# A recurrent attention and FFN kernel: denominators by bank, a reordered first layer norm, one load for V, the last layer norm on another engine, other banks in the FFN

## The chip, the cores and the metric

The kernel runs on one core of one Trainium2 chip. The metric is the device time of one execution in microseconds (us); lower is better. The times quoted are medians of executions that the measurement calls fast. A ratio is the mean time of one kernel's fast runs over the mean time of the other's fast runs of the same rounds, so it is not quite the ratio of the medians that stand beside it. Traces are of single executions, and a number from a trace is a number of that execution.

## The reference, cut to what matters

One sequence of 2048 tokens, width 512. It is layer-normalised and cut into 64 segments of 32 tokens. Each segment attends, with 32 heads of 128, over itself and 8 memory rows, and the first 8 rows of its output are the memory of the next segment. So segments run strictly one after the other. A second layer norm and a gated FFN (512 to 1376 to 512, ReLU gate) follow.

```python
for s in range(n_seg):                                   # 64, serial
    h = jnp.concatenate([mem, xs], axis=1)               # 8 + 32 rows
    q = jnp.einsum('btd,dhe->bhte', h, Wq)               # k, v alike
    scores = jnp.einsum('bhqe,bhke->bhqk', q, k) * scale
    p = _softmax(jnp.where(mask, scores, -1e9))
    o = jnp.einsum('bhqk,bhke->bhqe', p, v)
    o = jnp.einsum('bhte,hed->btd', o, Wo)
    mem = o[:, :M, :].copy()
...
h = x + A(layernorm(x));  h2 = h + B(layernorm(h))       # B: (relu(gate) * up) @ W_down
```

## The kernel before

The program is written as one list of instructions for each engine, with waits on named events of other engines. An engine works through its own list in order, so the place of an instruction in its list matters as much as its waits. The five places below are those that the change touches (cuts are marked with `...`). `mm` is a TensorE matmul, `act` a ScalarE (ACT) instruction, `e_tt`/`e_stt`/`e_copy` are elementwise ones on VectorE (DVE) or GpSimd (POOL). A bank is one of the pieces of PSUM, the memory that matmuls write to; `psf(b, ...)` is bank b.

The start. Four chunks of 512 tokens are transposed, their sums and squares are formed on TensorE, and all chunks are normalised only after the last of them:

```python
for c in range(NCH):
    ...                                     # 16 transposes, copies to HT (ACT and DVE)
    e_tt("dve", SQ, src_all(c), src_all(c), ALU.mult, ...)
    ...                                     # 4 + 4 matmuls with ONES: sums, sums of squares
    act(A1, psf(bS1, 0, CH), ACT.Square, ..., scale=1.0 / D_MODEL)
    e_stt("dve", VV, psf(bS2, 0, CH), 1.0 / D_MODEL, A1, ALU.mult, ALU.subtract, ...)
    act(VV, VV, ACT.Ln, ...);  act(RB[c], VV, ACT.Exp, ..., scale=-0.5)
    e_stt("dve", MRB[c], psf(bS1, 0, CH), 1.0 / D_MODEL, RB[c], ALU.mult, ALU.mult, ...)
prev = [("dve", "1MR%d" % (NCH - 1))]
for c in range(NCH):
    for tau in range(4):                    # 2 x 4 x 4 = 32 DVE instructions
        e_tt("dve", TTb, src_tau(c, tau), RB[c], ALU.mult, ..., waits=prev)
        ...
```

The middle of a segment on TensorE. V is made in four chunks of 512 columns; its matmuls use half the array's columns each (`tile_position`), the others use the whole array:

```python
emit_v_chunk(0, ...);  emit_pairs(...)                   # V chunk 0, then the scores
emit_v_chunk(1, [("dve", "QE%db1" % s)])
for b in range(3):                                       # softmax denominators
    w = [("dve", "MK%db2" % s)] if b == 0 else []        # all behind the third mask
    mm(psf(b, 0, SCOLS[b]), ONES, EB[:, 480 * b:480 * b + SCOLS[b]], True, True,
       post=(("pe", "D%d" % s) if b == 2 else None), waits=w)
emit_v_chunk(2, [("dve", "QE%db2" % s)])
emit_v_chunk(3, [("dve", "VE%dc0" % s)])
...                                                      # O = P V (16), then Wo (128)
```

ACT makes the reciprocals as exp(-ln(x)), in two pieces (960 and 320 columns). DVE's list in a segment is: evict Q, evict V chunk 0, three masks, evict V chunks 1, 2 and 3, scale O by the reciprocals in three pieces, residual add. The FFN accumulates the first half of the down projection in banks 0 and 1 and then the second half in the same banks:

```python
for fc in range(NFC):
    for k, dc in enumerate((2, 3)):
        w = [("dve", "RA%d" % c)] if (fc == 0 and k == 0) else []   # banks 0, 1 must be read out
        mm(PSF[:, 512 * (dc - 2):512 * (dc - 2) + CH], WDv[...], HFFv[...], ...)
```

The second layer norm of each segment runs on GpSimd, one segment behind; that of the last segment has nothing to hide behind. The V weights are loaded in eight pieces that sort the heads into even and odd, in runs of 256 bytes.

The softmax here doesn't subtract the row's maximum and nothing guards it: scores larger than these inputs give would overflow.

Of the kernel before, what the change touches and what calls it, by code (L numbers as in the profile page):

```python
# [3 lines left out]
P = 128  # L4
# [9 lines left out]
SEGL = 32  # L14
# [60 lines left out]
def build_kernel(nc, A_x, A_mem0, A_Wq, A_Wk, A_Wv, A_Wo, A_seg_len, B_x, B_W_gate, B_W_up, B_W_down, out):  # L75
# [16 lines left out]
    with ExitStack() as es:  # L92
# [40 lines left out]
        WVv = WBUF[:, OFF_V:OFF_V + 16384].rearrange("p (t b q e) -> p t b q e", t=4, b=2, q=16)  # L133
# [82 lines left out]
        wv5 = A_Wv.rearrange("(t p) (q b) e -> t b p q e", p=P, b=2)  # L216
        for b in range(2):
            for tau in range(4):
                dma("sp", WVv[:, tau, b, :, :], wv5[tau, b], post=("d_wv", "w%d%d" % (b, tau)))
# [23 lines left out]
        for c in range(NCH):  # L243
            first = True
            for t_ in range(TPC):
                for tau in range(4):
                    w = []
                    if first:
                        w = [("d_x%d" % c, "x"), ("gp", "ID1")]
                        if c > 0:  # L250
                            w += [("act", "XTE%da" % (c - 1)), ("dve", "XTE%db" % (c - 1))]
                        first = False
                    tr(PSH[:, tau * 512 + t_ * 128:tau * 512 + t_ * 128 + 128],
                       xr_tiles(c)[:, t_, tau * 128:(tau + 1) * 128], ID[:, :],
                       post=(("pe", "XT%d" % c) if (t_ == TPC - 1 and tau == 3) else None), waits=w)
            act(HT[:, 0:2, c * CH:(c + 1) * CH],
                PSH[:, 0:1024].rearrange("p (t c) -> p t c", t=2)[:, :, 0:CH], ACT.Copy,
                post=("act", "XTE%da" % c), waits=[("pe", "XT%d" % c)])
            e_copy("dve", HT[:, 2:4, c * CH:(c + 1) * CH],
                   PSH[:, 1024:2048].rearrange("p (t c) -> p t c", t=2)[:, :, 0:CH],  # L260
                   post=("dve", "XTE%db" % c), waits=[("pe", "XT%d" % c)])
            par = c % 2
            bS1, bS2 = 2 * par, 2 * par + 1
            w = [("act", "XTE%da" % c), ("dve", "XTE%db" % c)]
            if c > 0:
                w.append(("pe", "1S2c%d" % (c - 1)))
            e_tt("dve", SQ[:, :, :], src_all(c), src_all(c), ALU.mult, post=("dve", "1SQ%d" % c), waits=w)
            for tau in range(4):
                w = []
                if tau == 0:  # L270
                    w = [("act", "XTE%da" % c), ("dve", "XTE%db" % c), ("gp", "ONE")]
                    if c >= 2:
                        w.append(("dve", "1MR%d" % (c - 2)))
                mm(psf(bS1, 0, CH), ONES[:, :], src_tau(c, tau), tau == 0, tau == 3,
                   post=(("pe", "1S1c%d" % c) if tau == 3 else None), waits=w)
            for tau in range(4):
                w = [("dve", "1SQ%d" % c)] if tau == 0 else []
                mm(psf(bS2, 0, CH), ONES[:, :], SQ[:, tau, :], tau == 0, tau == 3,
                   post=(("pe", "1S2c%d" % c) if tau == 3 else None), waits=w)
            w = [("pe", "1S1c%d" % c)]  # L280
            if c > 0:
                w.append(("dve", "1V%d" % (c - 1)))
            act(A1, psf(bS1, 0, CH), ACT.Square, post=("act", "1A1%d" % c), waits=w, scale=1.0 / D_MODEL)
            e_stt("dve", VV, psf(bS2, 0, CH), 1.0 / D_MODEL, A1, ALU.mult, ALU.subtract,
                  post=("dve", "1V%d" % c),
                  waits=[("pe", "1S2c%d" % c), ("act", "1A1%d" % c)])
            act(VV, VV, ACT.Ln, post=("act", "1L%d" % c), waits=[("dve", "1V%d" % c), ("gp", "EPS")],
                bias=EPSB[:, 0:1])
            act(RB[c], VV, ACT.Exp, post=("act", "1R%d" % c), waits=[("act", "1L%d" % c)], scale=-0.5)
            e_stt("dve", MRB[c], psf(bS1, 0, CH), 1.0 / D_MODEL, RB[c], ALU.mult, ALU.mult,  # L290
                  post=("dve", "1MR%d" % c), waits=[("act", "1R%d" % c)])
        prev = [("dve", "1MR%d" % (NCH - 1))]
        for c in range(NCH):
            for tau in range(4):
                e_tt("dve", TTb, src_tau(c, tau), RB[c], ALU.mult, post=("dve", "1T%dt%d" % (c, tau)),
                     waits=prev)
                o = XNT4[:, tau, c * SPC:(c + 1) * SPC, 0:32]
                e_tt("dve", o, TTb.rearrange("p (s c) -> p s c", c=32)[:, 0:SPC, :],
                     MRB[c].rearrange("p (s c) -> p s c", c=32)[:, 0:SPC, :], ALU.subtract,
                     post=("dve", "1N%dt%d" % (c, tau)), waits=[("dve", "1T%dt%d" % (c, tau))])  # L300
                prev = [("dve", "1N%dt%d" % (c, tau))]
        for tau in range(4):
# [36 lines left out]
        def emit_ln2_act_lr(q):  # L339
            i = q % 2  # L340
            w = [("gp", "V2%d" % q), ("gp", "EPS")]
# [6 lines left out]
        def emit_ln2_gp(q):  # L348
            i = q % 2
            e_tt("gp", M2SQ[i], MEAN2[i], MEAN2[i], ALU.mult, post=("gp", "V2a%d" % q),  # L350
                 waits=[("act", "CP2%d" % q)] + ([("gp", "N2%dt3" % (q - 1))] if q > 0 else []))
            e_tt("gp", VV2[i], EX2B[i], M2SQ[i], ALU.subtract, post=("gp", "V2%d" % q), waits=[("gp", "V2a%d" % q)])
            e_tt("gp", MR2b[i], MEAN2[i], R2b[i], ALU.mult, post=("gp", "MR2%d" % q),
                 waits=[("act", "R2%d" % q), ("gp", "V2%d" % q)])
            prev = [("gp", "MR2%d" % q)]
            for tau in range(4):
                e_tt("gp", TT2b[i], HT[:, tau, q * SEGL:(q + 1) * SEGL], R2b[i], ALU.mult,
                     post=("gp", "T2%dt%d" % (q, tau)), waits=prev)
                e_tt("gp", XNT4[:, tau, q, 0:32], TT2b[i], MR2b[i], ALU.subtract,
                     post=("gp", "N2%dt%d" % (q, tau)), waits=[("gp", "T2%dt%d" % (q, tau))])  # L360
                prev = [("gp", "N2%dt%d" % (q, tau))]

        for s in range(NSEG):
# [35 lines left out]
            def emit_v_chunk(cv, waits_first=()):  # L399
                vb = Vbank[cv]  # L400
                first = True
                for tau in range(4):
                    for b in range(2):
# [3 lines left out]
                           WVv[:, tau, b, 4 * cv:4 * cv + 4, :], tau == 0, tau == 3,  # L407
# [9 lines left out]
            emit_v_chunk(0, ([("d_wv", "w13")] if s == 0 else []) + [("dve", "QE%db0" % s)])  # L417
# [4 lines left out]
            for b in range(3):  # L422
                w = [("dve", "MK%db2" % s)] if b == 0 else []
                mm(psf(b, 0, SCOLS[b]), ONES[:, :], EB[:, 480 * b:480 * b + SCOLS[b]], True, True,
                   post=(("pe", "D%d" % s) if b == 2 else None), waits=w)
            emit_v_chunk(2, [("dve", "QE%db2" % s)])
            emit_v_chunk(3, [("dve", "VE%dc0" % s)])
# [29 lines left out]
            for b in range(3):  # L457
                act(EB[:, 480 * b:480 * b + SCOLS[b]], psf(b, 0, SCOLS[b]), ACT.Exp,
                    post=("act", "EX%db%d" % (s, b)), waits=[("pe", "S%db%d" % (s, b))], scale=SCALE)
            act(LR[:, 0:960].rearrange("p (b c) -> p b c", b=2), PSF3[:, 0:2, 0:480], ACT.Ln,  # L460
                post=("act", "LN%da" % s), waits=[("pe", "D%d" % s)])
            act(LR[:, 0:960], LR[:, 0:960], ACT.Exp, post=("act", "RC%da" % s), waits=[("act", "LN%da" % s)],
                scale=-1.0)
            act(LR[:, 960:1280], psf(2, 0, 320), ACT.Ln, post=("act", "LN%db" % s))
            act(LR[:, 960:1280], LR[:, 960:1280], ACT.Exp, post=("act", "RC%db" % s),
                waits=[("act", "LN%db" % s)], scale=-1.0)
# [5 lines left out]
            if last:  # L472
                emit_ln2_act(s)
                emit_ln2_act_lr(s)
# [26 lines left out]
            for b in range(3):  # L501
                w = [("pe", "O%db%d" % (s, b)), ("act", "RC%d%s" % (s, "a" if b <= 1 else "b"))]
# [12 lines left out]
            if last:  # L515
                emit_ln2_gp(s)
# [6 lines left out]
        def ffn_chunk(c):  # L523
# [4 lines left out]
            for fc in range(NFC):  # L528
# [6 lines left out]
                for tau in range(4):  # L535
                    w = []
                    if tau == 0:
                        if fc == 0 and c == 0:
                            w = [("gp", "N2%dt3" % (NSEG - 1)), ("d_ffn", "d1"),
                                 ("act", "CP2%d" % (NSEG - 1))]  # L540
                        if gi >= 2:
# [3 lines left out]
                for tau in range(4):  # L545
                    w = [("dve", "HF%d" % (gi - 2))] if (tau == 0 and gi >= 2) else []
                    mm(PSF[0:rows, 512 * ub:512 * ub + CH], WUv[:, tau, fc * 128:fc * 128 + rows], hnt(c, tau),
# [8 lines left out]
                if fc >= 1:  # L556
                    pf = fc - 1
                    prow = rows_of(pf)
                    for k, dc in enumerate((0, 1)):
                        w = []  # L560
                        if k == 0:
                            w = [("dve", "HF%d" % gis[pf])]
                            if pf == 0 and c > 0:
                                w.append(("dve", "RB%d" % (c - 1)))
# [9 lines left out]
            for fc in range(NFC):  # L574
                rows = rows_of(fc)
                for k, dc in enumerate((2, 3)):
                    w = [("dve", "RA%d" % c)] if (fc == 0 and k == 0) else []
                    mm(PSF[:, 512 * (dc - 2):512 * (dc - 2) + CH], WDv[0:rows, fc, dc * 128:(dc + 1) * 128],
# [4 lines left out]
            e_tt("dve", HT[:, 2:4, c * CH:(c + 1) * CH], PSF3[:, 0:2, 0:CH], HT[:, 2:4, c * CH:(c + 1) * CH], ALU.add,  # L583
# [107 lines left out]
```

## Time and profile before

| | before |
|---|---|
| median of the first 5 runs | 1350.24 us (1344.64 to 1352.33) |
| profiled run | span 1344.6 us |
| start, until the first K matmul | 50.6 us |
| 64 segments and hand-over, until the first FFN matmul | 1156.4 us |
| FFN and output | 137.6 us |

TensorE is busy for nine tenths of the span. What a change can gain is in what it waits for, so the rows to look at are TensorE's groups with their idle time, and of those the one of the denominators (the moving operand is SMALL, the stationary one ONES). After the bar stand busy time and mean; after the second bar the idle time just before the group, and what ended it ("issue", in later lines, is idle time for which the profile shows nothing that was waited for):

```profile
PE 1200.8 (89%) x30059; PEld 900.3 (67%) x30071; DVE 552.1 (41%) x1060; ACT 464.7 (35%) x1029; POOL 180.0 (13%) x723
...
L155 PE MATMUL PSF<-SMALL,ONES 128*128 128x32 bf16 (+3 forms) x464 | 69.4, 263 | 31.1 <-DVE SMALL L167 30.9
```

The 31.1 us are the 64 waits for the third mask, 0.48 us each.

### The profile page before, as it was taken

What the parts mean: (1) busy time and instruction counts of PE and PEld (TensorE: products, weight loads), DVE (VectorE), ACT (ScalarE), POOL (GpSimd) and SP (SyncE); (2) the same over time, 40 slices, a digit from 0 to 9 for tenths busy, and PEclk for the clock granted to TensorE, in tenths of its full rate; (3) what the DMA queues carried; (4) which work ended last, traced back from release to release, by engine and by line L of the source; (5) the groups of instructions that cost most, each with busy time, mean ns of one, the idle gap of its engine ahead of it and who ended that gap; (6) DMA issues with size and microseconds to landing.
All of it is one profiled execution on the core that took longest, in us unless ns stands there. A gap on an engine that the chain in (4) does not pass through costs nothing.

```text
span 1344.6 us, 63817 instructions
## 1 busy us (share of the span) xinstructions
PE 1200.8 (89%) x30059; PEld 900.3 (67%) x30071; DVE 552.1 (41%) x1060; ACT 464.7 (35%) x1029; POOL 180.0 (13%) x723
## 2 busy tenths in 40 slices
PE   5499999999999999999999999999999999979996
PEld 2377777777777777777777777777777777754443
DVE  3543444443434444434444444444444444433332
ACT  3133333333333333333333333333333333332222
POOL 1001111111111111111111111111111111120000
PEclk8699999999999999999999999999999999999998
DMA  9900000000000000000000000000000000030000
GB/s 343 220 4 4 3 3 3 4 3 4 4 4 3 3 3 4 3 4 4 4 3 3 3 4 4 3 4 3 3 4 3 4 3 3 3 129 1 17 16 32
DMA packets 27879, 29.29 MB, mean 22 GB/s; under 512 B 16760, under 2 KB 25312, under 8 KB 26592
## 3 DMA queue, kind: packets, MB, share of 16 engines
q1 hardware_dynamic: 27328, 24.16, 5.8%
q8 instruction: 235, 3.85, 1.2%
q0 software_dynamic: 288, 1.05, 0.2%
q14 instruction: 28, 0.23, 0.1%
HBM read 23.11 MB, written 2.10 MB: 19 GB/s over the span
## 4 chain that ended last, share of the span: by engine, by line
PE 75%; DVE 11%; ACT 7%; issue 4%; DMA 0%; POOL 0%; DVEq 0%; POOLq 0%; ACTq 0%
PE PSF L155 75%; DVE SMALL L167 8%; ACT SMALL L161 5%; DVE SMALL L164 1%; ACT XNT L161 1%; DVE BT L167 1%; DVE XNT L167 1%; DVE HT L167 0%; ACT FTMP L161 0%; ACT WBUF L161 0%; DMA out_dram<-WBUF 0%; DVE WBUF L167 0%; PE PSH L158 0%; DVEq L645 0%; POOL BT L167 0%
## 5 line engine op out<-in xcount | busy, mean ns | idle before, releaser
L155 PE MATMUL PSF<-XNT,WBUF 128*128 128x40 bf16 (+1 forms) x16736 | 518.0, 184 | 27.2 <-ACT XNT L161 18.2
L155 PEld LDWEIGHTS PSF<-XNT,WBUF 128*128 128x128 bf16 x16736 | 456.2, 96 | 77.3 <-ACT XNT L161 24.8
L164 DVE CAST SMALL<-PSF 128x512 bf16<-128x512 f32 (+2 forms) x448 | 292.1, 652 | 446.6 <-PE PSF L155 438.5
L161 ACT ACTIVATE SMALL<-PSF 128x480 bf16<-128x480 f32 (+1 forms) x384 | 188.3, 526 | 406.4 <-PE PSF L155 406.4
L155 PE MATMUL PSF<-WBUF,XNT 128*40 128x512 bf16 x2048 | 256.5, 383 | 0.0
L155 PE MATMUL PSF<-SMALL,WBUF 128*128 128x40 bf16 x8192 | 235.4, 180 | 21.7 <-DVE SMALL L167 15.8
L155 PEld LDWEIGHTS PSF<-SMALL,WBUF 128*128 128x128 bf16 x8192 | 220.3, 96 | 38.7 <-DVE SMALL L167 36.8
L155 PEld LDWEIGHTS PSF<-WBUF,XNT 128*40 128x40 bf16 x2048 | 89.4, 99 | 99.9 <-DVE SMALL L164 21.1
L161 ACT ACTIVATE FTMP<-PSF 128x32 f32<-128x32 f32 (+3 forms) x260 | 109.3, 449 | 86.3 <-PE PSF L155 86.3
L167 POOL TENSOR_TENSOR BT<-FTMP,BT 128x32 bf16<-128x32 f32 x64 | 15.8, 246 | 902.0 <-ACT BT L161 902.0
L155 PEld LDWEIGHTS PSF<-SMALL 128*128 128x128 bf16 x2048 | 81.8, 100 | 79.1 <-DVE SMALL L164 78.2
L155 PE MATMUL PSF<-SMALL 128*128 128x80 bf16 x2048 | 107.2, 204 | 16.2 <-DVE SMALL L164 16.2
L167 DVE TENSOR_TENSOR HT<-PSF,HT 128x128 bf16<-128x128 f32 (+1 forms) x72 | 28.5, 395 | 223.2 <-ACT XNT L161 197.4
L167 DVE TENSOR_TENSOR SMALL<-PSF,FTMP 128x480 bf16<-128x480 f32 (+1 forms) x192 | 102.9, 591 | 0.0
L161 ACT ACTIVATE XNT<-PSF 128x32 bf16<-128x32 f32 x63 | 12.4, 198 | 260.2 <-PE PSF L155 260.2
L155 PE MATMUL PSF<-SMALL,ONES 128*128 128x32 bf16 (+3 forms) x464 | 69.4, 263 | 31.1 <-DVE SMALL L167 30.9
L161 ACT ACTIVATE FTMP<-FTMP 128x960 f32<-128x960 f32 (+1 forms) x128 | 94.3, 737 | 4.1
L155 PEld LDWEIGHTS PSF<-SMALL,ONES 128*128 128x128 bf16 x464 | 26.3, 98 | 73.7 <-DVE SMALL L167 64.4
L167 DVE TENSOR_TENSOR SMALL<-SMALL,MASKF 128x480 bf16<-128x480 bf16 (+1 forms) x192 | 68.0, 381 | 18.1 <-ACT SMALL L161 14.7
L167 POOL TENSOR_TENSOR XNT<-BT 128x32 bf16<-128x32 bf16 x256 | 63.0, 246 | 20.0
L167 POOL TENSOR_TENSOR BT<-HT,BT 128x32 bf16<-128x32 bf16 x256 | 63.0, 246 | 20.0
L167 DVE TENSOR_TENSOR WBUF<-WBUF,PSF 128x512 bf16<-128x512 bf16 (+1 forms) x44 | 30.2, 688 | 69.4 <-PE PSF L155 64.9
(39 smaller groups left out, 277.9 us busy)
## 6 DMA issues: line engine op xcount, KB each, us to landing
WBUF<-in_A_Wk_dram SPq DMA_DIRECT2D x1, 4096.0 KB, 16.4
WBUF<-in_A_Wq_dram SPq DMA_DIRECT2D x1, 4096.0 KB, 27.2
WBUF<-in_A_Wv_dram SPq DMA_DIRECT2D x8, 512.0 KB, 7.5
WBUF<-in_A_Wo_dram SPq DMA_DIRECT2D x1, 4096.0 KB, 17.6
out_dram<-WBUF SPq DMA_DIRECT2D x4, 512.0 KB, 2.9
WBUF<-in_B_W_gate_dram SPq DMA_DIRECT2D x1, 1376.0 KB, 6.4
WBUF<-in_B_W_up_dram SPq DMA_DIRECT2D x1, 1376.0 KB, 9.5
WBUF<-in_B_W_down_dram SPq DMA_DIRECT2D x1, 1280.0 KB, 12.3
```

The lines of the kernel that those rows point to most:

```text
L155: E.matmul(o, l, r, start=st, stop=sp, **kw), post, waits)
L161: add("act", lambda E, o=out, i=in_, f=func, kw=kw: E.activation(out=o, in_=i, func=f, **kw), post, waits)
L164: add(eng, lambda E, o=out, i=in_: E.tensor_copy(o, i), post, waits)
L167: add(eng, lambda E, o=out, a=in0, b=in1, op_=op: E.tensor_tensor(out=o, in0=a, in1=b, op=op_), post, waits)
```

## The change

Its intent: take waits out of TensorE's list. Five edits, the diff cut to its core:

```diff
 # 1. denominators by bank, each behind its own mask; reciprocals by bank
-            for b in range(3):
-                w = [("dve", "MK%db2" % s)] if b == 0 else []
-                mm(psf(b, 0, SCOLS[b]), ONES[:, :], EB[...], True, True, post=... , waits=w)
-            emit_v_chunk(2, [("dve", "QE%db2" % s)])
+            emit_den(0)                      # waits MK b0
+            emit_v_chunk(2, [("dve", "QE%db2" % s)])
+            emit_den(1)                      # waits MK b1
+            emit_den(2)                      # waits MK b2
             emit_v_chunk(3, [("dve", "VE%dc0" % s)])
...
-            act(LR[:, 0:960]..., PSF3[:, 0:2, 0:480], ACT.Ln, ...)     # and Exp, then 320 columns
+            for b in range(3):
+                act(lr, psf(b, 0, SCOLS[b]), ACT.Ln, ..., waits=[("pe", "D%db%d" % (s, b))])
+                act(lr, lr, ACT.Exp, ..., scale=-1.0)
 # 2. the start: one chunk's statistics and normalisation beside the next chunk's transposes
+        p0_xte_dve(0)
+        for c in range(1, NCH):
+            p0_xte_dve(c)                    # copy and square of chunk c
+            p0_vmr_norm_dve(c - 1)           # variance, mean term, 8 normalisation steps of c-1
+        p0_vmr_norm_dve(NCH - 1)
...                                           # TensorE and ACT lists reordered alike
 # 3. V weights in natural order, one load
-        for b in range(2):
-            for tau in range(4):
-                dma("sp", WVv[:, tau, b, :, :], wv5[tau, b], ...)
+        dma("sp", WBUF[:, OFF_V:OFF_V + 16384]..., A_Wv.rearrange("(t p) h e -> p t (h e)", p=P), ...)
-                           WVv[:, tau, b, 4 * cv:4 * cv + 4, :], tau == 0, tau == 3,
+                           WVn[:, tau, 4 * cv:4 * cv + 4, b, :], tau == 0, tau == 3,
 # 4. second layer norm of the last segment on DVE instead of GpSimd
-                emit_ln2_gp(s)
+                emit_ln2_gp(s, eng="dve")
 # 5. FFN: second half of the down projection in banks 4, 5
-                    w = [("dve", "RA%d" % c)] if (fc == 0 and k == 0) else []
-                    mm(PSF[:, 512 * (dc - 2):...
+                    w = []
+                    mm(PSF[:, 512 * (dc + 2):...
...                                           # the next chunk's first "up" matmul waits for the second add
```

## The prediction

> **What bounds the kernel now.** I read the chain that ended last first, to see which engine sets the end, then the timeline of one segment, of the start, of the hand-over to the FFN and of an FFN chunk, then the DMA view by window.
>
> ```profile
> PE 75%; DVE 11%; ACT 7%; issue 4%; DMA 0%; POOL 0%; DVEq 0%; POOLq 0%; ACTq 0%
> ```
>
> TensorE carries the end; DVE and ACT have a share only where TensorE stands and waits for them. So the change is worth what it shortens of those waits. In the timeline the first K matmul of segment 1 starts at 73.03 us and that of segment 2 at 90.87: a period of 17.84 us, 64 times, 1142 of the 1344.6 us. The middle of segment 1:
>
> ```profile
> 81.38 1.04 PE L155 MATMUL PSF<-WBUF,XNT 128*40 128x512 bf16 x8
> 81.73 1.12 DVE L167 TENSOR_TENSOR SMALL<-SMALL,MASKF 128x480 bf16<-128x480 bf16 x3 [0.23 <-ACT SMALL L161]
> ...
> 82.91 0.71 PE L155 MATMUL PSF<-SMALL,ONES 128*128 128x480 bf16 x3 [0.48 <-DVE SMALL L167]
> ...
> 83.55 1.91 PE L155 MATMUL PSF<-WBUF,XNT 128*40 128x512 bf16 x16
> ...
> 84.64 0.69 DVE L164 CAST SMALL<-PSF 128x512 bf16<-128x512 f32 x1 [1.19 <-PE PSF L155]
> ...
> 85.50 0.69 DVE L164 CAST SMALL<-PSF 128x512 bf16<-128x512 f32 x1 [0.17 <-PE PSF L155]
> ...
> 86.11 1.61 DVE L167 TENSOR_TENSOR SMALL<-PSF,FTMP 128x480 bf16<-128x480 f32 x3
> ...
> 86.81 3.77 PE L155 MATMUL PSF<-SMALL,WBUF 128*128 128x40 bf16 x128 [0.25 <-DVE SMALL L167]
> ```
>
> Read it as a chain: V chunk 1 (81.38), the three denominator matmuls (82.91, released by the end of the third mask, 81.73 + 1.12 = 82.85), V chunks 2 and 3 (83.55), the eviction of chunk 3 (85.50), the first scaling of O (86.11), the Wo matmuls (86.81). The scaling starts when that eviction ends, not when O or the reciprocal is there: the reciprocal of the first two banks was written at 85.66. So the end of V chunk 3 on TensorE sets when Wo starts.
>
> Start, hand-over and FFN:
>
> ```profile
> 48.80 0.43 DVE L167 TENSOR_TENSOR XNT<-BT 128x512 bf16<-128x512 bf16 x1
> ...
> 49.37 1.44 PE L155 MATMUL PSF<-WBUF,ONES 128*128 128x512 bf16 x3 [17.54 <-DVE XNT L167]
> ...
> 60.22 0.69 PE L155 MATMUL PSF<-XNT,WBUF 128*128 128x40 bf16 x16 [2.77 <-issue]
> ```
> ```profile
> 1207.01 5.27 PE L155 MATMUL PSF<-XNT,WBUF 128*128 128x512 bf16 x16 [4.55 <-POOL XNT L167]
> ...
> 1234.48 4.92 PE L155 MATMUL PSF<-WBUF 128*128 128x512 bf16 x21 [1.32 <-DVE HT L167]
> ```
>
> TensorE waits 17.54 us for the last normalisation, then stops once more for 2.77 us with nothing but "issue" ahead of it, while the Wo load is running (the DMA rate falls from 341 to 79 GB/s at 60 to 61 us, when TensorE resumes). It waits 4.55 us for GpSimd before the FFN, and 1.32 us in each of four chunks for the first residual add.
>
> **What the Trainium skill says.** "TensorEngine Tiling (Array Packing)", Key Properties: changing the tiling mode drains TensorE. V is column-tiled (40 wide at two positions), the denominators are not. The trace agrees and gives the size: V pairs start 0.216 us apart (84.21, 84.43), but from the last pair's start (85.08) to the O matmul (85.39) it is 0.31, and from the last denominator (83.32, 320 columns, some 0.135) to V it is 0.23. So a switch costs about 0.095 us. "DMA: Bandwidth & Descriptors", Specifications: at least 512 B per transfer for line rate. The trace agrees: in the window 30 to 50 us, nearly all packets (15,300 of 15,936) are under 512 B and 228 GB/s flow; before it 375 to 416. "Runtime: NRT & Kernel Launch", Instruction fetch mechanics: each engine's instructions are refilled by DMA in 16 KiB blocks. The 2.77 us fit that (one instruction packet lands in 61 to 62), but no line proves it. "TensorE: Matmul & The Clock Gate": idle time re-throttles the clock; here the FFN's first 9 weight loads are 0.43 us apart, later matmuls 0.216. I give no gain for it.
>
> **Part 1, denominators by bank (each segment).** Removed: the wait for the third mask. Added: one more full/tiled round trip, two switches. Moved: denominators 1 and 2 behind V chunk 2. A V chunk is 4 x 0.216 + 0.095 = 0.96 us to the next full matmul; a 480-column denominator 0.2025.
> - Denominator 0 needs mask 0 (81.73 + 0.41 = 82.14, plus 0.06 as seen for mask 2) and chunk 1 with its switch: 81.38 + 0.96 = 82.34. The second is later.
> - V chunk 2: 82.34 + 0.2025 + 0.095 = 82.64 (before 83.55).
> - Denominators 1 and 2: 82.64 + 0.96 = 83.60; masks long done (82.85).
> - V chunk 3: 83.60 + 0.34 + 0.095 = 84.03 (before 84.43).
>
> So chunk 3, its eviction, the scaling and Wo come 0.39 us earlier: 64 x 0.39 = 25 us. Does ACT keep up? Its two logarithms and exponentials become three of each. From the rows 0.42 (320 columns) and 0.97 (960), 480 columns cost about 0.56 for the logarithm; from 0.47 and 1.00, 0.60 for the exponential. Reciprocal 0 is then ready at about 83.95, 1 at 85.2, 2 at 86.1; the scalings want them at 85.7, 86.3, 86.9. ACT pays 0.35 us a segment more, off the path.
>
> **Part 2, the start.** DVE is in order. Before: four rounds of 6.73 us (V at 11.49, 18.22, 24.94, 31.67), then 32 normalisation steps of 0.46 us from 34.54. After, chunk by chunk on DVE: copy 0.69, square 1.23, variance 0.69, wait for ACT, mean term 0.69, normalisation 8 x 0.46 = 3.68. The ACT wait is now square 0.60 (of the next chunk, which is queued ahead) + Ln 0.72 + Exp 0.63 + gaps = 2.1 us. A round is then 9.1 us. Placing them: copy 0 at 6.78, first variance at about 14.1, normalisation 0 ends 21.3, 1 at 30.5, 2 at 39.6; the last round, with nothing to overlap, ends at about 46.2. Before: 49.2. Gain 3.0 us, less than the name "pipelined" suggests, since the in-order DVE now waits on ACT.
>
> The V weights: 4.19 MB at about 400 instead of 228 GB/s take 10.5 instead of 18.5 us, so all loads end at about 52 instead of 60.5. TensorE did not wait for V (60.84, right behind Q), so this gains nothing by itself; but the 2.77 us stop came 6.8 us after the first K matmul, at 57.45. Now that place is about 54.5, after the loads. I take the stop as gone: 3.0 + 2.8 = 5.8 us. V's moving operand becomes strided in 128-element runs; the FFN's moving operand has 32-element runs and still shows 0.216 us a matmul, so no cost.
>
> **Part 3, last layer norm on DVE.** Eleven GpSimd steps of 128x32 at 0.325 us become DVE steps. From 0.225 us (128x128) and 0.426 (128x512) I estimate 0.17, with the gap 0.21: gain 11 x 0.115 = 1.25 us. But the last piece of the down weights, issued at 1193.2, takes 12.4 us, so it lands at 1205.6, and TensorE would otherwise start at 1207.01 - 0.39 - 1.25 = 1205.4. I take 1.0 us.
>
> **Part 4, FFN banks.** The wait of 1.32 us goes in four chunks: 5.3 us. In exchange the next chunk's first "up" matmul waits for the second add: from 1239.44 for 1.22, so free at 1240.72, wanted after four gate matmuls at 1239.24 + 0.86 = 1240.10: 0.6 us lost once. Later chunks have the 16 output transposes in between (about 0.9 us), which cover it. Gain 4.7 us.
>
> Sum: 25 + 5.8 + 1.0 + 4.7 = 36.5; from 1350.2 that is 1314.
>
> **Rivals.** (a) The switches cost more than 0.095 us when they stand between short groups; at 0.2 us each the two extra ones eat 0.2 of the 0.39, leaving some 12 us, and the time is about 1327. For it: the V0-to-scores switch shows 0.25 us of idle TensorE; against it: the start-to-start times above already contain that. (b) DVE becomes the bound: masks, evictions and scalings are one queue. Against it: DVE idles 1.19 us ahead of the eviction at 84.64. If it were so, the segments gain nothing: 1339. (c) The fetch stop stays, because it needs traffic and not only that traffic: 1317. (d) Reciprocals late on ACT, now in three pieces: the margin is 0.8 us at the smallest; if it fails, some 0.2 us a segment, 1327.
>
> **Range and chances.** The segments hold two thirds of the gain, and 0.1 us of error there is 6.4 us; the start is uncertain by 3, the base by 3. I predict 1315 us, 8 in 10 between 1307 and 1326. The 2% line is at about 1323. Faster 0.8, within 2% 0.19, slower 0.01.
>
> **What would show it.** A period of about 17.45 us; the first denominator 0.96 us behind V chunk 1 with no wait for masks; one denominator, then V, then two, and V chunk 3 about 2.65 us behind chunk 1. First K matmul about 3 us earlier and no "issue" stop of 2.8 us; loads over by 52 us. No 1.32 us wait in the FFN, one wait of about 0.6 us at the second chunk's up matmul. I am wrong if the period stays above 17.7, if TensorE waits for ACT ahead of Wo, or if V matmuls with the natural layout are over 0.216 us apart.

## The result, and the profile after

| | before | after |
|---|---|---|
| median | 1352.14 us (1344.64 to 1354.61, 15 runs) | 1314.58 us (1312.6 to 1317.62, 8 runs) |
| ratio, 95% interval | | 0.9732 (0.9713 to 0.975) |
| span of the profiled run | 1344.6 us | 1313.2 us |
| median period of a segment | 17.85 us | 17.52 us |

The period is the time from one segment's copy of the memory rows (ACT, XNT<-PSF) to the next one's, of 62 such steps of a trace.

The page of the changed kernel, the rows that answer to those of before, and its chain that ended last:

```profile
PE 1209.9 (92%) x30059; PEld 895.7 (68%) x30071; DVE 553.7 (42%) x1071; ACT 488.2 (37%) x1157; POOL 176.1 (13%) x712
...
PE 84%; DVE 6%; issue 5%; ACT 2%; DMA 0%; DVEq 0%; ACTq 0%
...
L155 PE MATMUL PSF<-SMALL,ONES 128*128 128x32 bf16 (+3 forms) x463 | 78.1, 258 | 0.1
```

The wait ahead of the denominators has gone to the last tenth, 31.1 to 0.1 us, and TensorE carries 84% of the chain instead of 75%; ACT's share falls from 7% to 2% although ACT works 23 us more. But the period fell by 0.33 us and not by 0.48, so part of the 31 us came back elsewhere. The timeline of one segment shows where:

```profile
93.10 1.04 PE L155 MATMUL PSF<-WBUF,XNT 128*40 128x512 bf16 x8
93.45 1.12 DVE L167 TENSOR_TENSOR SMALL<-SMALL,MASKF 128x480 bf16<-128x480 bf16 x3 [0.23 <-ACT SMALL L161]
...
94.08 0.38 PE L155 MATMUL PSF<-SMALL,ONES 128*128 128x480 bf16 x1
...
94.38 1.04 PE L155 MATMUL PSF<-WBUF,XNT 128*40 128x512 bf16 x8
...
95.36 0.51 PE L155 MATMUL PSF<-SMALL,ONES 128*128 128x480 bf16 x2
...
95.80 1.04 PE L155 MATMUL PSF<-WBUF,XNT 128*40 128x512 bf16 x8
...
97.50 1.61 DVE L167 TENSOR_TENSOR SMALL<-PSF,FTMP 128x480 bf16<-128x480 f32 x3
...
98.20 2.96 PE L155 MATMUL PSF<-SMALL,WBUF 128*128 128x40 bf16 x96 [0.24 <-DVE SMALL L167]
```

Denominator 0 starts 0.98 us behind V chunk 1 and waits for nothing; V chunk 3 starts 95.80 - 93.10 = 2.70 us behind chunk 1. Before, it was 84.43 - 81.38 = 3.05. From chunk 3 to Wo it is 2.40 us here and was 2.38.

The start and the FFN of the changed kernel, in time order:

```profile
44.91 1.44 PE L155 MATMUL PSF<-WBUF,ONES 128*128 128x512 bf16 x3 [10.98 <-DVE XNT L167]
...
46.15 3.65 PE L155 MATMUL PSF<-XNT,WBUF 128*128 128x40 bf16 x112
...
51.77 4.61 PE L155 MATMUL PSF<-XNT,WBUF 128*128 128x40 bf16 x144 [1.97 <-issue]
```
```profile
1179.85 6.39 PE L155 MATMUL PSF<-XNT,WBUF 128*128 128x512 bf16 x16 [3.35 <-DVE XNT L167]
...
1206.51 5.36 PE L155 MATMUL PSF<-WBUF 96*128 96x512 bf16 x23 [0.42 <-DVE WBUF L167]
...
1213.19 2.76 PE L155 MATMUL PSF<-XNT,WBUF 128*128 128x512 bf16 x12 [0.46 <-DVE HT L167]
```

The stop marked "issue" is still there, now after 112 matmuls instead of 240. The second half of the down projection follows the first without a wait (23 matmuls in one group), and the price is the wait of 0.46 us of the second chunk's "up" matmuls.

Where the two traces part, from their timelines:

| point of the trace | before, us | after, us | gained up to here |
|---|---|---|---|
| first K matmul | 50.60 | 46.15 | 4.45 |
| first V matmul | 60.84 | 56.30 | 4.54 |
| first K matmul of segment 1 | 73.03 | 67.12 | 5.91 |
| memory rows copied, segment 62 | 1183.37 | 1158.02 | 25.35 |
| first FFN matmul | 1207.01 | 1179.85 | 27.16 |
| first matmul of FFN chunk 1 | 1239.24 | 1211.71 | 27.53 |
| end | 1344.6 | 1313.2 | 31.4 |

Two of these rows do not fit the prediction: the stop did not go, so the step from the first K to the first V gained almost nothing; and FFN chunk 0 gained 0.37 us where 1.32 had been expected (as will be seen, this second figure is one of this pair of traces). The experiments look at these and at the segment.

### The profile page after: what moved, and what is told of

It reads as the page before. It is cut to its first block, busy times and chain, and to the rows that moved or that the text cites. A ratio compares the mean times of both kernels' runs of the same rounds, so it can differ in the third digit from the quotient of the medians.

```text
span 1313.2 us, 63940 instructions
## 1 busy us (share of the span) xinstructions
PE 1209.9 (92%) x30059; PEld 895.7 (68%) x30071; DVE 553.7 (42%) x1071; ACT 488.2 (37%) x1157; POOL 176.1 (13%) x712
## 3 DMA queue, kind: packets, MB, share of 16 engines
q8 instruction: 235, 3.85, 1.2%
## 4 chain that ended last, share of the span: by engine, by line
PE 84%; DVE 6%; issue 5%; ACT 2%; DMA 0%; DVEq 0%; ACTq 0%
PE PSF L155 84%; DVE SMALL L167 5%; ACT XNT L161 1%; ACT FTMP L161 0%; DVE BT L167 0%; ACT WBUF L161 0%; DVE XNT L167 0%; DMA out_dram<-WBUF 0%; DVE WBUF L167 0%; PE PSH L158 0%; DVE SMALL L164 0%; ACT BT L161 0%; DVE HT L167 0%; DVEq L685 0%; DVE BT L172 0%
## 5 line engine op out<-in xcount | busy, mean ns | idle before, releaser
L155 PE MATMUL PSF<-WBUF,XNT 128*40 128x512 bf16 x2048 | 267.8, 382 | 0.4 <-issue 0.3
L155 PEld LDWEIGHTS PSF<-WBUF,XNT 128*40 128x40 bf16 x2048 | 83.8, 99 | 99.7 <-issue 22.2
L161 ACT ACTIVATE FTMP<-PSF 128x32 f32<-128x32 f32 (+3 forms) x324 | 120.2, 394 | 42.7 <-PE PSF L155 30.7
L161 ACT ACTIVATE FTMP<-FTMP 128x480 f32<-128x480 f32 (+1 forms) x192 | 107.2, 558 | 6.1
L155 PE MATMUL PSF<-SMALL,ONES 128*128 128x32 bf16 (+3 forms) x463 | 78.1, 258 | 0.1
```

Source lines behind the costliest of these rows:

```text
L155: E.matmul(o, l, r, start=st, stop=sp, **kw), post, waits)
L161: add("act", lambda E, o=out, i=in_, f=func, kw=kw: E.activation(out=o, in_=i, func=f, **kw), post, waits)
```

## The experiments

The theories. **A**: the start of V chunk 3 on TensorE sets when Wo starts, and each switch between column-tiled and full matmuls costs about 0.1 us. **F**: the "issue" stops of the first K and Q matmuls are blocks of TensorE's instructions that come late because the weight loads fill the DMA queues. **C**: FFN chunk 0 was slow since TensorE's clock was halved for longer. Each has its rival in the expectations. Every run was correct.

| run | what it is | median, us (before beside it) | ratio to before, 95% | median period, us |
|---|---|---|---|---|
| c_before | before again | 1351.02 (1350.41) | 0.9997 (0.9972 to 1.0022) | 17.85 |
| e_den | part 1 alone | 1330.34 (1350.41) | 0.9844 (0.9825 to 0.9863) | 17.52 |
| e_rest | all but part 1 | 1335.78 (1350.41) | 0.9892 (0.9875 to 0.9908) | 17.85 |
| e_v12 | change, all denominators behind V chunk 2 | 1312.56 (1350.41) | 0.9721 (0.9705 to 0.9736) | 17.49 |
| e_d3 | change, all denominators ahead of V chunk 2 | 1309.77 (1349.21) | 0.9694 (0.9671 to 0.9718) | 17.44 |
| e_pipe | reordered start alone | 1348.67 (1349.21) | 0.9983 (0.9954 to 1.0011) | 17.85 |
| e_wv | V layout and load alone | 1346.17 (1349.21) | 0.9961 (0.9934 to 0.9988) | 17.85 |
| e_wohold | change, Wo loaded later | 1322.36 (1349.21) | 0.979 (0.977 to 0.981) | 17.52 |
| c_after | change again | 1313.25 (1351.35) | 0.9718 (0.9701 to 0.9736) | 17.52 |
| x_pipe2 | change, start overlapped further | 1313.26 (1351.35) | 0.9714 (0.9697 to 0.9731) | 17.52 |
| x_warm | change, idle matmuls ahead of the FFN | 1310.64 (one run) | one look | 17.52 |
| x_best | e_d3, x_pipe2 and x_warm together | 1306.21 (1351.35) | 0.9663 (0.9646 to 0.9681) | 17.44 |

### The control

No edit.

> The kernel before, unchanged, as a control and for a second profile. Expected: a ratio within 0.3% of 1; the median segment period again 17.85 us. Theory A (the part of a segment that is over the median, 3.9 us summed over 62 segments in the profile of before, differs from run to run and makes the spread of 1344 to 1354 us): the second profile shows another sum of such excess, 4 to 12 us, and its time moves with it. Rival: the sum is again 3.9 +- 0.5 us and the spread comes from the start or the end.

Ratio 0.9997, period 17.85. The time that the segments spent over the median period came to 4.2 us. That is the rival's figure and also the low edge of theory A's range, so the control does not separate them; and the execution that was profiled was the quickest of its four (1345.12 us, the others 1350 to 1353), so it says nothing of a slow one. The control is inconclusive. One number goes with the time: the mean granted clock of TensorE was 0.983 in the quickest execution and 0.978 to 0.980 in the other three. The spread of before matters below: both traces of before are of executions some 6 us under the median of their kernel.

### Part 1 alone, and all but part 1

e_den is the first block of the diff on the kernel before; e_rest is the changed kernel with that block undone.

> The kernel before with part 1 alone (denominators by bank, reciprocals by bank). Theory A (V chunk 3 on TensorE sets when Wo starts): median period 17.52 instead of 17.85 us, V chunk 3 2.70 us behind V chunk 1 instead of 3.05, time 21 us less than before (ratio 0.984, 0.982 to 0.987). Rival (part 1 needs the other parts, or its gain is mostly fewer irregular stops): period above 17.7, ratio above 0.990.

> The changed kernel with part 1 undone (the three denominators again behind the third mask, reciprocals again in two pieces); start, last layer norm and FFN banks as changed. Theory A: the parts add, so this gains what is left: period 17.85 us, start about 5.9 us, hand-over 1.3, FFN 4.2 less, together 11.4, ratio 0.9915 (0.989 to 0.994). Rival (the parts are not additive, since the start is hidden behind something else): ratio above 0.995.

The segment of e_den, its TensorE rows:

```profile
101.66 1.04 PE L155 MATMUL PSF<-WBUF,XNT 128*40 128x512 bf16 x8
...
102.64 0.38 PE L155 MATMUL PSF<-SMALL,ONES 128*128 128x480 bf16 x1
...
104.36 1.04 PE L155 MATMUL PSF<-WBUF,XNT 128*40 128x512 bf16 x8
```

Chunk 3 is 2.70 us behind chunk 1 and the period is 17.52, both as theory A had them, and with nothing else changed; the ratio 0.9844 is in its range. e_rest has the old period, and its ratio is at the edge of the range, on the better side. As savings: (1 - 0.9844) and (1 - 0.9892) of 1350.4 us are 21.1 and 14.6, together 35.7; the whole change saves (1 - 0.9732) x 1352 = 36.2. The parts add to within the noise (each interval is some 2.5 us to either side), and part 1 is about six tenths of the gain.

### Is it the mask waits, or moving denominators behind chunk 2?

The change does two things to the denominators at once. e_d3 keeps the waits and undoes the moving; e_v12 moves all three.

```diff
 # e_d3                                        # e_v12
 emit_den(0)                                   emit_v_chunk(2, ...)
+emit_den(1)                                  +emit_den(0)
+emit_den(2)                                   emit_den(1)
 emit_v_chunk(2, ...)                          emit_den(2)
 emit_v_chunk(3, ...)                          emit_v_chunk(3, ...)
```

> The changed kernel with the three denominators in one group ahead of V chunk 2 again, each waiting for its own mask (as before the change in place, as in the change in waits). It tells the mask wait from the placing. Theory A: denominators 0 and 1 run while mask 2 is being made, denominator 2 is released at 1.53 us behind V chunk 1 (where all three were released before), V chunk 2 follows at 1.76, V chunk 3 at 2.62 (2.70 in the change, 3.05 before), since one round trip of switches is gone; reciprocals in time; period 17.45 instead of 17.52, time 4 to 5 us less than the changed kernel. Rival (moving two of the denominators behind chunk 2 is what pays): V chunk 3 later than 2.8, period 17.65 or more.

> The changed kernel with all three denominators behind V chunk 2 instead of one before and two behind it: TensorE goes V chunk 1, V chunk 2, denominators 0, 1, 2, V chunk 3, so the extra round trip between column-tiled and full matmuls (two switches) is gone, and V chunks 1 and 2 have none between them. Theory A (each extra switch costs about 0.095 us and V chunk 3 sets the start of Wo): V chunk 3 starts 2.48 us behind V chunk 1 instead of 2.70, but the reciprocals start about 0.9 us later, so the third scaling waits for ACT for some 0.1 us; period 17.52 - 0.13 = 17.39 (17.30 to 17.45), time 8 us less than the changed kernel, ratio to before 0.967. Rival (a switch costs nothing by itself, or ACT's reciprocals become the bound): V chunk 3 2.6 us or more behind chunk 1, or a wait of 0.25 us or more of DVE for ACT at the scaling; period 17.52 or more.

TensorE in e_d3:

```profile
92.77 1.04 PE L155 MATMUL PSF<-WBUF,XNT 128*40 128x512 bf16 x8
...
93.75 0.86 PE L155 MATMUL PSF<-SMALL,ONES 128*128 128x480 bf16 x3
...
94.54 1.91 PE L155 MATMUL PSF<-WBUF,XNT 128*40 128x512 bf16 x16
```

Chunk 2 starts 94.54 - 92.77 = 1.77 us behind chunk 1 (expected 1.76). Chunk 3 follows 4 x 0.216 = 0.86 later, at 2.63 (expected 2.62), and the period is 17.44. So waiting for each mask by itself is what pays. The third denominator is still released by the third mask, but by then the other two are done, so only the third (320 columns) still stands between the third mask and V chunk 2. Moving two of them behind V chunk 2 costs 0.07 to 0.08 us a segment, the extra round trip between array modes less the wait that it avoids. The rival falls. The two ratios, 0.9694 and 0.9732, are of different rounds and their intervals overlap a little, so the claim that e_d3 is the quicker of the two rests on the periods, 62 steps of each trace.

In e_v12, TensorE does still better, and the time does not:

```profile
93.84 1.91 PE L155 MATMUL PSF<-WBUF,XNT 128*40 128x512 bf16 x16
...
96.33 1.04 PE L155 MATMUL PSF<-WBUF,XNT 128*40 128x512 bf16 x8
...
98.02 1.79 DVE L167 TENSOR_TENSOR SMALL<-PSF,FTMP 128x480 bf16<-128x480 f32 x3
...
98.75 0.47 ACT L161 ACTIVATE FTMP<-FTMP 128x320 f32<-128x320 f32 x1
```

Chunk 3 is 2.49 us behind chunk 1, as expected (2.48), 0.21 better than in the change. But the last reciprocal is ready at 98.75 + 0.47 = 99.22, so the scaling takes 1.79 instead of 1.61 us: the third piece waits about 0.18 for ACT. The period came to 17.49, not 17.39: of 0.21 us gained on TensorE, 0.18 went into the wait for ACT; the time, 1312.56 us, is 2 us under the change's instead of 8, and the two are not told apart. Theory A was right about TensorE, and half of the rival (ACT becomes the bound) was right about the time. Here moving the denominators back stops paying: the reciprocals, 3.2 us of ACT work in a row (0.57 + 0.60 twice, 0.42 + 0.47), need them early.

### The stop in the first K and Q matmuls

e_pipe and e_wv are the second and third blocks of the diff, each alone on the kernel before. e_wohold is the changed kernel with one wait more:

```diff
         dma("sp", WOv[:, :, :], A_Wo.rearrange("h e d -> e h d"), post=("d_wo", "w"),
+            waits=[("pe", "Q0b2")])
```

> The kernel before with the start reordered as in the change (software pipelining of the first layer norm), but the V weights still loaded in eight pieces with 256 B packets and nothing else changed. Theory F (TensorE's stop in the first K and Q matmuls is a 16 KiB block of its instructions that comes late because the weight loads fill the DMA queues): first K matmul at 46.1 us as in the changed kernel, but the loads now last to 60.5 us, so both block boundaries (after 112 and after 240 matmuls) fall under them and TensorE stops at both, 3 to 7 us together; V chunk 0 at 57 to 60 us, total gain 1 to 4 us, ratio 0.997 to 0.999. Rival (the stop does not depend on the loads): one stop of about 2 us, V chunk 0 at 56.3, gain 4.5 us, ratio 0.9965.

> The kernel before with the V weights in natural layout and one load of 8 KB runs, nothing else. Theory F: first K matmul still at 50.6 us, all loads over by about 51, so the blocks come in time: no stop over 1 us, or only at the first boundary, and V chunk 0 at 58 to 59 instead of 60.8; gain 2 to 3 us, ratio 0.998 (0.996 to 1.000). V matmuls still 0.216 us a pair, period 17.85. Rival (the stop does not depend on the loads): stop of 2 us or more, V chunk 0 at 60.5 or later, no gain. Rival two (the strided moving operand slows V): period above 17.9.

> The changed kernel, with the load of Wo held back until the last Q matmul of segment 0, so that no weights are loading while the first K and Q run. Theory F: no stop over 0.5 us between the first K matmul (44.9 + 1.2) and V chunk 0, which then starts about 2 us earlier (54 instead of 56.3); Wo lands about 12 us after the last Q, at 66, so the first Wo matmul waits for it, some 4 to 5 us later than the 63.06 us of the changed kernel; time 1 to 5 us more. Rival (the stop is of the instruction stream or clock alone): a stop of about 2 us stays after 112 matmuls although nothing loads.

First e_pipe, then e_wv, then e_wohold:

```profile
46.34 3.69 PE L155 MATMUL PSF<-XNT,WBUF 128*128 128x40 bf16 x112
51.16 3.35 PE L155 MATMUL PSF<-XNT,WBUF 128*128 128x40 bf16 x128 [1.13 <-issue]
57.90 0.69 PE L155 MATMUL PSF<-XNT,WBUF 128*128 128x40 bf16 x16 [3.39 <-issue]
```
```profile
50.47 7.47 PE L155 MATMUL PSF<-XNT,WBUF 128*128 128x40 bf16 x256
```
```profile
46.83 7.44 PE L155 MATMUL PSF<-XNT,WBUF 128*128 128x40 bf16 x256
...
69.37 4.42 PE L155 MATMUL PSF<-SMALL,WBUF 128*128 128x40 bf16 x128 [8.67 <-DMA WBUF<-in_A_Wo_dram]
```

All three stopped, or did not stop, as theory F had it. With the loads lasting to 60 us (e_pipe) TensorE stops twice, and the two places are 128 matmuls apart, which with their weight loads are 256 instructions. The page of before counts 235 packets and 3.85 MB on its larger instruction queue, so 16.4 KB a packet, and (3.85 + 0.23) MB for 63,817 instructions, so 64 bytes each: one packet holds 256 instructions. With the loads over early (e_wv), or held back (e_wohold), all 256 matmuls run through. The DMA view by windows of 1 us fits. In the first trace of the change a packet of 16 KB of the instruction queue stands in the window from 49 to 50 us (it begins at 49.1 and takes 1.2 us), and the stop ends at 51.77; in e_pipe such packets begin in the windows from 48 and from 55 us, two to three microseconds before each stop ends. The starts of before differ in the same way: with a packet that begins at about 31 us (both traces of before) there is one stop, without one ahead of 52 us (e_den) there are two.

The times: e_pipe 0.9983, not told from 1, with the first V at 58.52 us (2.3 earlier); e_wv 0.9961, the first V at 57.86 (3.0 earlier, a little better than expected), with the period still at 17.85, so a strided V operand costs nothing that shows and that rival falls. The reorder alone runs into the loads. That the two start edits help each other is not shown: 2.3 and 3.0 alone make 5.3, and both together brought the first V 4.5 us earlier in the first trace of the change and 6.9 in c_after. In e_wohold the first V came at 54.20, 2.1 us earlier than in the change, but Wo then kept TensorE 8.67 us, and the time was 8 us more, not 1 to 5 as expected: Wo landed some 15 us after its release instead of 12.

c_after and x_pipe2 add to this. x_pipe2 fills DVE's wait for ACT in the start:

```diff
-            p0_xte_act(c);  p0_stat_act(c);  p0_lr_act(c - 1)
+            p0_xte_act(c);  p0_lr_act(c - 1);  p0_stat_act(c)
...
-            p0_xte_dve(c)                   # copy and square
-            p0_vmr_norm_dve(c - 1)
+            p0_xte_dve(c);  p0_v_dve(c - 1)
+            p0_sq_dve(c)                    # in the wait for ACT
+            p0_mr_norm_dve(c - 1)
```

> The changed kernel again, as a control on the chip of this batch and for a second profile. Expected ratio 0.973 (0.971 to 0.976), period 17.52 us, stop of 1.5 to 2 us after 112 matmuls, and the half clock at the FFN's start again for 3.4 to 6 us (its length depends on where the throttle's window lies, so it need not be the 5.7 us of the first profile).

> The changed kernel with the start pipelined further: on DVE the next chunk's square goes behind the variance, into the wait for ACT, and on ACT the logarithm and exponential go ahead of the next chunk's square, so the wait of 2.0 us for ACT in each of three rounds is filled. DVE then ends the last normalisation about 3 x 1.8 = 5.4 us earlier, and the first K matmul starts at about 40.7 instead of 46.15. Theory F (the weight loads, over at 51 us, delay the instruction blocks): TensorE now stops at both block boundaries, 112 and 240, for 4 to 7 us together, and V chunk 0 starts at 52 to 55 instead of 56.3: under half of the 5.4 us is kept, or little more, ratio 0.971 to 0.973. Rival (stops are of fixed length about 2 us): V chunk 0 at 51 or before, the whole 5.4 us kept, ratio 0.969.

First c_after, then x_pipe2:

```profile
46.70 7.35 PE L155 MATMUL PSF<-XNT,WBUF 128*128 128x40 bf16 x256
```
```profile
41.73 3.52 PE L155 MATMUL PSF<-XNT,WBUF 128*128 128x40 bf16 x112
47.03 4.20 PE L155 MATMUL PSF<-XNT,WBUF 128*128 128x40 bf16 x128 [1.78 <-issue]
53.22 0.55 PE L155 MATMUL PSF<-XNT,WBUF 128*128 128x40 bf16 x16 [1.99 <-issue]
```

x_pipe2 starts K at 41.73, 1 us later than expected but 4.4 us earlier than the first trace of the change; it stops at both boundaries for 3.8 us in all (expected 4 to 7), and makes the first V matmul at 53.71, 2.6 earlier. Against c_after, measured in the same rounds, nothing is left (0.9714 and 0.9718). Work pulled forward into the loads was given back to the loads, as theory F said.

c_after was a miss: the same program, loads as long as before, and no stop at all. Its trace has a packet of the instruction queue landing already in the window from 34 us, and so has x_warm, which has no stop either. The four traces with this start that do stop (the change, e_rest, e_v12, e_d3: 1.97, 1.68, 1.86, 1.57 us) have none before the window from 49 or 50. e_wohold shows that a late block is not enough: its packet comes only at 46.6 us, behind the long wait too, but with nothing loading it is over in 0.9 us and TensorE does not stop. So whether a program stops depends on whether one block was fetched before TensorE's long wait or after it, under the loads, and the same program does both. What decides that is open.

### FFN chunk 0

```diff
             if last:
                 emit_ln2_stats_pe(s)
+                for _ in range(14):
+                    mm(psf(0, 0, 512), ONES[:, :], MASKF[:, 0:512], True, True)
```

> The changed kernel with 14 idle matmuls of 512 columns (on constants, into a free bank) between the last layer-norm statistics and the FFN, which take about 14 x 0.216 = 3.0 of the 3.35 us that TensorE stands there. Theory C (FFN chunk 0 gained only 0.4 us instead of 1.3 because TensorE ran at half clock for 5.7 us after the pause, against 3.4 us in the kernel before): no half clock at the FFN's start, its first matmuls 0.216 us apart, chunk 0 takes 31.86 - 2.8 = 29.1 us from its first matmul to that of chunk 1 (28.8 to 29.6). Rival (the first chunk is slow for another reason, the late weights or ACT and DVE): half clock gone, chunk 0 still 31 us or more.

The windows view gives the granted clock as a share of full speed in the third column from the right. First before, then the change, then x_warm, each from the start of its FFN:

```profile
1209.00:1210.00 1.00, 1.00 (x4) 0.33 (x3) 0.00 (x0) 0.53 (x1) 0.00 (x0) 0.50 0.00 0
1210.00:1211.00 1.00, 1.00 (x5) 0.42 (x4) 0.34 (x1) 0.00 (x0) 0.00 (x0) 0.81 0.00 0
```
```profile
1184.00:1185.00 1.00, 1.00 (x4) 0.36 (x3) 0.24 (x1) 0.00 (x0) 0.00 (x0) 0.50 0.00 0
1185.00:1186.00 1.00, 1.00 (x5) 0.44 (x4) 0.00 (x0) 0.60 (x1) 0.00 (x0) 0.76 0.00 0
```
```profile
1178.20:1179.20 1.00, 0.91 (x5) 0.44 (x6) 0.03 (x1) 0.00 (x0) 0.00 (x0) 1.00 0.00 0
```

Before, the half clock ended 3.4 us after the first FFN matmul (1207.01 to about 1210.4). In the change, with a shorter pause ahead of it, it ended after 5.7 us (1179.85 to about 1185.5), which costs (5.7 - 3.4) / 2 = 1.15 us more. In c_after it ended after 5.2 us (1177.78 to about 1183.0), so the longer half clock is in both traces of the change. It is not the change's doing, though. In e_v12 and e_wohold, with the same FFN, the half clock ended 3.3 and 3.7 us after the first FFN matmul; in e_pipe and e_wv, with the FFN of before and its pause of 4.55 us, after 4.9 and 5.2. Over the twelve traces without idle matmuls it is 3.0 to 6.0 us. In each trace the clock's changes lie 3.41 us apart or a whole multiple of that, so it fits that the length depends on where in such a stretch the FFN begins. Chunk 0 takes 32.0 to 34.9 us in the five traces with the FFN of before, 33.2 in the mean, and 30.7 to 32.0 in the seven with that of the change, 31.4 in the mean: the 0.37 us of the first pair is at the low end.

The clock has a second part in the FFN of before. In e_pipe and e_wv, and not in before, c_before and e_den, it is halved once more for 3.4 us behind the wait for the residual add, in chunk 0 and in the last chunk. The last chunk in before, then in e_pipe:

```profile
1328.20 4.92 PE L155 MATMUL PSF<-WBUF 128*128 128x512 bf16 x21 [1.32 <-DVE HT L167]
```
```profile
1331.89 6.61 PE L155 MATMUL PSF<-WBUF 128*128 128x512 bf16 x21 [1.32 <-DVE HT L167]
```

The same 21 matmuls take 1.7 us more. From its first matmul to the end, the FFN takes 141.7 and 141.9 us in these two traces and 137.4 to 137.6 in the three others. None of the nine traces with the new banks, where the waits of 1.32 us are gone, has such a stretch. That the wait makes it is argued: before, c_before and e_den have the same wait without it.

Back to x_warm. With idle matmuls in the pause the clock is full from the first one. Chunk 0 then takes 29.1 us, from 1178.29 to the first matmul of chunk 1, which stands 1.48 us ahead of the "up" group at 1208.86 as it does in the change (1211.71 and 1213.19); expected 29.1, and 31.86 in the change. So theory C holds for the trace that it was made for, and there the pause cost 2.8 us of clock besides its own length. x_warm is a single run; its time is no evidence by itself.

### All that helped

The three edits shown above on one kernel.

> All that helped together: the changed kernel with the three denominators in one group, each behind its own mask, the further pipelined start, and the 14 idle matmuls ahead of the FFN. If the parts add: period 17.44 (62 x 0.08 = 5 us less than the change), start 1 to 3 us less, FFN chunk 0 2.7 us less: 1304 us, ratio 0.966 (0.963 to 0.969). If the start gives nothing: 0.967 to 0.968.

1306.21 us, ratio 0.9663 (0.9646 to 0.9681), against 0.9718 (0.9701 to 0.9736) for the change in the same rounds. It beats both kernels, by 45 and 7 us. The ratio is the 0.966 that was expected; the time is 2.2 us over the 1304.

## Why the prediction was right

It said 1315 us and 36.5 us of gain; measured are 1314.58 and, by the ratio, 36.2. Its steps are less exact than that.

- **The chain of a segment** (V chunk 3 sets Wo): right, shown by e_den, e_d3 and e_v12, which each moved V chunk 3 by a different amount and moved the start of Wo with it.
- **Its size**, 0.39 us: too large; it measured 0.33 (17.85 to 17.52). The term is the V chunk with its switch: 0.98 us both times, not 0.96, and 0.30 for denominator 0 with its switch, as computed. So 64 segments give 21 us and not 25. Rival (a), switches of 0.2 us, falls; (b) and (d) did not occur in the change. (d) had the margin of 0.8 us that was computed: the third reciprocal is written at 97.80, and its scaling starts at 98.63. e_v12, where the denominators come later, uses it up.
- **The start, first half**, 3.0 us: it gained 4.45. The first variance came at 13.54 and not at 14.1, since TensorE's clock was already full there, and a round took 25.10 - 16.22 = 8.88 us from mean term to mean term, not 9.1.
- **The start, second half**, "I take the stop as gone": the step that failed in the first trace. The loads do end by about 51 us, and that does remove the stop (e_wv), but the stop moved with the work to an earlier block boundary, still under the loads, and lasted 1.97 us; TensorE then ran at half clock again (granted 0.50 from 53 to 55 us, where before had 1.00 from 54 to 57), 144 matmuls in 4.61 us, where before it had done 240 in 6.84. In c_after it was gone. The sum of both halves, predicted 5.8, is 4.54 in one trace and 60.84 - 53.98 = 6.86 in the other. Counted at the first K of segment 1, when a half clock that before still had from 60.1 to 63.5 us is over too, it is 5.6 and 7.9, part 1's 0.33 taken off. So in the first trace the 5.8 was right in size, by other steps than those of the sum. One reading under it was wrong: the packet "in 61 to 62" starts at 61.35, after TensorE resumed at 60.22; the one that fits the stop starts at 57.52.
- **Last layer norm**, 1.0 us: the wait fell from 4.55 to 3.35, so 1.2. The weights did not bind, but nearly: in e_d3, where the segment ends a little earlier still, TensorE waits 3.67 us and for the down weights.
- **FFN banks**, 4.7 us: the waits behaved as said (four of 1.32 gone, one of 0.46 come, predicted 0.6), and 31.4 - 27.16 = 4.24 were kept in this pair of traces, where the half clock cost 1.15 us more than before. The prediction saw the half clock and gave it nothing; over all traces it was no loss (see FFN chunk 0).

The terms of the first trace add to 31.4 us, the spans' own difference, not to 36. The rest is on the side of before: its two traced executions took 1346.27 and 1345.12 us, its median is 1352, while the traced execution of the change, 1314.97, is a median one. What a 1352 us execution of before does otherwise has no trace. The largest candidate is the clock in the FFN: with the two halved stretches behind the residual adds and a longer one at the start, the FFN of before was 4 us longer in two of five traces. The new banks leave no wait of 1.32 us, so against an execution like that the FFN gains some 8 us and not 4.2. The clocks fit: the mean granted clock was 0.982 and 0.983 in the two traced executions, and 0.980 or less in most of those over 1350 us. Two smaller ones were seen: e_den, whose start is that of before, made its first V at 62.33 us instead of 60.84, with both stops (1.39 and 3.40 us); and e_pipe, whose segments are those of before, spent 7.3 us over the median period, where the two traces of before spent 3.9 and 4.2. That these make the slow executions is argued, not shown. So the agreement of the total to half a microsecond is partly chance: an overestimate of 4 us in the segments and a base that was taken from the median stand against each other.

## What to carry to other kernels

Follow a wait to the instruction that it delays last, here V chunk 3, and count what stands in front of that one; the idle row said 0.48 us a segment, the chain 0.39, and 0.33 came. Splitting a wait by its pieces and moving the pieces are two edits, so try them apart: here the split gained 0.4 us and the moving lost 0.07. And before pulling work forward, see what else runs there: work moved under weight loads waited for its own instructions, and a pause of 3 us cost nearly as much again in clock. Last, compare more than one trace before a microsecond of one pair is explained: the clock alone moved FFN chunk 0 by up to 2.8 us between traces of the same FFN.

## What the Trainium skill lacked or had wrong

- "TensorEngine Tiling (Array Packing)", Key Properties, says that changing the tiling mode drains TensorE, without a size. Here a switch costs about 0.1 us: a V chunk of four pairs 0.216 us apart takes 0.98 us to the next full matmul (0.86 without a switch).
- "Runtime: NRT & Kernel Launch", Instruction fetch mechanics, has blocks of 256 instructions, as the traces show too, and calls the cost of crossing one mostly hidden. Under weight loads of about 350 GB/s it was not: stops of 1.1 to 3.4 us, 128 matmuls apart, gone when nothing loads or when the block had come early.
- "TensorE: Matmul & The Clock Gate", Part 1, gives about 3.4 us of work until the full clock, half a microsecond of variation, since the window runs free, and in the same part 6, 11 or 14 slow matmuls for one kernel. Here the half clock lasted 3.0 to 6.0 us past the first matmul of the FFN in twelve traces, at about 0.43 us a matmul: the counts fit, the half microsecond is too little.
- "DMA: Bandwidth & Descriptors", Why small descriptors are slow (HBM only), works out an overhead of 27% for a descriptor of 256 B, and names 32 B of metadata for each besides. An estimate from both figures is 11/8 x 288/256 = 1.55 times the time. Here it was more: the V weights went at 216 GB/s in packets of 256 B (before) and at 419 in packets of 8 KB (the change), 1.94 times the time.
- No page says that a block of instructions may be fetched before or after a long wait in the same program: here at 34 us in two traces of this start, at 49 to 50 in four.
